# RWKV6 attention with an MLP on one core: round 0 turned by back-to-back transposes, and later rounds' w, k and r fetched in runs of steps and turned on VectorE

## The chip, the core and the metric

The kernel runs on one NeuronCore of a Trainium2 chip. A core has a matrix engine (TensorE, "PE" in the profile; its weight loads are "PEld"), a vector engine (VectorE, "DVE"), a scalar engine (ScalarE, "ACT"), a general engine (GpSimd, "POOL") and a queue engine (SyncE, "SP") that issues most transfers between HBM and the on-chip memory SBUF. 16 DMA engines carry the transfers. [...] Each engine runs its own instructions in order, and engines wait for one another by semaphores. The metric is device time in microseconds, the median of the runs of a kernel.

## The reference

The inputs r, k, v and w are float32 of [4 batches, 8 heads, 768 steps, 48 dimensions]. Attention is a recurrence over steps, followed by a layer norm and an MLP on 384 = 8 x 48 features:

```python
for t in range(S):
    kt, vt, rt, wt = (k[:, :, t], v[:, :, t], r[:, :, t], w[:, :, t])
    cur = np.einsum('bhd,bhe->bhde', u[None] * kt, vt)
    y[:, :, t] = np.einsum('bhd,bhde->bhe', rt, state + cur)
    state = wt[:, :, :, None] * state + np.einsum('bhd,bhe->bhde', kt, vt)
...
x = np.ascontiguousarray(attn_out.transpose(0, 2, 1, 3)).reshape(B, S, H * D)
xn = (x - mu) / np.sqrt(var + 1e-06) * g_ln
ch = np.maximum(xn @ w_ch1, 0.0) @ w_ch2
return (x + ch).astype(np.float32)
```

w_ch1 is [384, 1536] and w_ch2 is [1536, 384]. They arrive in float64, 8 bytes an element.

## The kernel before

The work is cut into 8 rounds, one for each batch and half of its 768 steps. A round has two units, one for each group of 4 heads, so a unit is 4 heads x 384 steps, and units 2n and 2n+1 belong to round n. Units 0 and 1 are round 0.

For the recurrence the kernel needs r, k and w with dimensions on the partitions and steps along the row: two heads share the 128 partitions, one from 0 and one from 64, so each tensor of a unit consists of two pairs of heads, each [128, 384]. In HBM the steps come first, so each pair has to be turned. `load` (L122) brings a tensor of a unit with steps on the partitions into a padded tile `nat` (three transfers of [128, 4, 48] each), and `turned` (L306) turns one pair: three PE transposes of 128x128 into PSUM and one copy to SBUF by ACT, into `wT` or `rkT`. For round 0 the rows are loaded by `load_rows` (L133) so that a partition holds three consecutive steps, and `turned` uses two 64-row products with the identity for each third of a pair. A product of float32 runs as two instructions on PE, a transpose as one.

A round then goes through six levels (0 to 5). In each, `quads` (L416) forms the products of k with r between neighbouring blocks of 1, 2, 4 ... 32 steps for both units (`a_ps`, 96 instructions), `grow` (L436) multiplies r and k by the decays that have come up to that block size (DVE, in place in `rkT`, so it waits for the level's products), and `keep` (L453) puts the wanted products into the matrix A by a mask. `totals` makes the decays by pairwise products of w. After level 5, `ends` turns k back (`kn`), `finish` copies the remainder, `states` (L509) makes the states at block ends (`kv` on PE, a chain on DVE), and `own_outputs` and `outputs` (L550, L565) give y. The term with u is r*k*u summed over dimensions: in rounds 0 and 1 by `products` (an elementwise product r*k, written `ruk`) and `product_sums` (PE, with u as the other side), later by `own_products` and `own_sums` from the untouched `nat` tiles; `own_term` multiplies it by v. DVE adds y and this term to x.

`moments` and `norm` (L602, L612) make xn, `turned_x` (L628) turns it (`xT`), and `mlp` (L640) is a generator of 24 steps of six PE instructions each: 12 for the hidden rows h (ACT applies the ReLU), and 12 for the output, whose sum with x DVE adds before SP stores it. The MLP of a round runs in the levels of the next two rounds.

The order on PE, ACT, DVE and POOL is the order in which the program states the calls. Transfers issued through `SP` are placed in the queue by a scheduler with its own estimate of the time; those through `SPO` keep the program's order. In the main loop, over `rnd` and `lev`, a level first does the states or outputs of the previous round, then `quads`, `grow` and `keep`; then `fill` (L697) deals the level's list of tasks out among MLP steps. `UNTIL` says how many MLP steps are done at the end of each level. Among the tasks are the turns of the next round: in round 2 at levels 3 to 5, in later rounds at levels 1 to 3, in the order w of both units, k and r of the first unit, k and r of the second. `norm` is a task of level 3, and `turned_x` of level 4.

The weights are converted while round 0 and 1 run: `fetch` brings a part in float64 words into one of four buffers with the tag "raw" ([128, 384, 2] words), `begin` (three ACT operations) takes it apart, and `join` (`shifted`, then `added`, on DVE) puts the float32 value together. The first MLP product needs three joined parts. `warm` issues idle products of zeros on PE between the steps of round 0.

Of the kernel before, what the change touches and what calls it, by code (L numbers as in the profile page):

```python
# [52 lines left out]
def kernel(  # L53
# [68 lines left out]
    def load(q, which="wkr", eng=SP):  # L122
        for nm in which:
            for c in range(TT):
                eng.dma_start(
                    out=nat[nm][q % 2][:, c, :, 0:D],
                    in_=steps({"w": w, "k": k, "r": r}[nm], q, c),
                )

    def flat(nm, q):  # L130
        return nat[nm][q % 2].rearrange("p c h d -> p (c h d)")

    def load_rows(nm, q, eng):  # L133

        b, f, g = units[q]
        src = {"w": w, "k": k, "r": r}[nm]
        eng.dma_start(
            out=flat(nm, q)[:, 0 : NH * TT * D].rearrange("p (h x) -> p h x", h=NH),
            in_=src[b, ts(g, NH), ds(f * RN, RN)].rearrange("h (p c) d -> p h (c d)", c=TT),
        )  # L140

    def load_v(q, eng=SP):
        vn[q] = p4.tile([P, TT, NH, D], F32, tag="v", name=f"v{q}")
# [148 lines left out]
    def warm(n, tag="m"):  # L292

        while n > 0:
            m = min(n, RN // P)
            ps = (ps_m if tag == "m" else ps_t).tile([P, RN], F32, tag=tag, name="idle")
            PE.matmul(
                ps[:, 0 : m * P], nought.broadcast_to([P, P]), nought.broadcast_to([P, m * P]),
                start=True, stop=True,
            )  # L300
            n -= m


    st, carry = {}, {}

    def turned(q, nm, pr):  # L306
        a = st.setdefault(q, {})
        if pr == 0:
            if nm == "w":
                if q % U == 0:  # L310
                    st["w"] = p1.tile([P, U, W], F32, tag="w", name=f"wT{q // U}")
                a["w"] = st["w"][:, q % U]
            elif "rk" not in a:

                rk = a["rk"] = p4.tile([P, 2, W], F32, tag="rkT", name=f"rkT{q}")
                a["r"], a["k"] = rk[:, 0], rk[:, 1]
        ps = ps_t.tile([P, RN], F32, tag="t", name=f"{nm}_ps{q}_{pr}")
        if q < U:

            for c in range(TT):  # L320
                for j in range(2):
                    at = ((2 * pr + j) * TT + c) * D
                    PE.matmul(
                        ps[ds(HP * j, HP), ts(c, P)], flat(nm, q)[:, ds(at, HP)], ident,
                        start=True, stop=True,
                    )
            ACT.copy(
                out=a[nm][:, ts(pr, RN)].rearrange("p (m c) -> p m c", c=TT),
                in_=ps.rearrange("p (c m) -> p m c", c=TT),
            )  # L330
            return
        for c in range(TT):
            PE.transpose(
                ps[:, ts(c, P)],
                nat[nm][q % 2][:, c, ts(pr, 2)].rearrange("p j d -> p (j d)"), ident,
            )
        ACT.copy(out=a[nm][:, ts(pr, RN)], in_=ps)
# [33 lines left out]

    def products(q, eng=DVE):
        a = st[q]
        if q < U:

            a["ruk"] = [
                p3.tile([P, RN], F32, tag="xn", name=f"ruk{q}_{pr}") for pr in pairs
            ]
            for pr in pairs:
                eng.tensor_tensor(  # L380
                    out=a["ruk"][pr], in0=a["r"][:, ts(pr, RN)], in1=a["k"][:, ts(pr, RN)],
                    op=ALU.mult,
                )
        else:
            ruk = p2.tile([P, NK, P], F32, tag="kn", name=f"ruk{q}")
            ruk = ruk.rearrange("p k t -> p (k t)")
            a["ruk"] = [ruk[:, ts(pr, RN)] for pr in pairs]
            eng.tensor_tensor(out=ruk, in0=a["r"], in1=a["k"], op=ALU.mult)

    def product_sums(q):  # L390
        b, f, g = units[q]
# [24 lines left out]
    def quads(q, lev):  # L416

        n = 1 << lev
        rnd, uu = divmod(q, U)
        if uu == 0:  # L420
            ps = ps_a.tile([P, 2, 512], F32, tag="a", name=f"a_ps{rnd}_{lev}")
            a_ps[rnd] = ps[:, :, 0 : W // 2].rearrange("s j (u k t) -> s j u k t", u=U, k=NK)
        K = st[q]["k"]
        R = st[q]["r"].rearrange("p (m q two n) -> p m q two n", m=NM, two=2, n=n)
        for c in range(NK):
            for i in range(2):
                for j in range(2):
                    m = 2 * c + i
                    rows = ds(HP * j, D)
                    PE.matmul(  # L430
                        a_ps[rnd][ds(C * (i ^ j), C), j, uu, c]
                        .rearrange("s (q n) -> s q n", n=n),
                        K[rows, ts(m, C)], R[rows, m, :, 1, :], start=True, stop=True,
                    )
# [301 lines left out]
    fetch(2)  # L736
    for nm in "wrk":
        run(each(turned, [u0], nm, pairs))
        warm(2)
    for nm in "wrk":  # L740
        POOL.memset(nat[nm][0][:, :, :, D:HP], 0.0)
    products(u0)
    quads(u0, 0)
    load(new[0], "wrk", SPO)
    grow(u0, 0)
    run(each(turned, [u1], "w", pairs))
    totals(0, DVE)
    warm(2)
    product_sums(u0)
    for nm in "rk":  # L750
        run(each(turned, [u1], nm, pairs))
        warm(2)
    for nm in "wrk":
        POOL.memset(nat[nm][1][:, :, :, D:HP], 0.0)
    products(u1)
# [3 lines left out]
    load_v(u0, SPO)  # L759
    load(new[1], "r", SPO)  # L760
    load_v(u1, SPO)
    load(new[1], "k", SPO)
    begin()
    begin()
    warm(3)
    grow(u1, 0)
    keep(0, 0)
    ahead = each(turned, new[:1], "wrk", pairs) + each(turned, new[1:], "wrk", pairs)
    for lev in range(1, NLEV):
        quads(u0, lev)  # L770
        quads(u1, lev)
        run(ahead[2 * lev - 2 : 2 * lev] if lev < NLEV - 1 else [])
        if lev in (2, 3):
            begin()
        warm(3 if lev < NLEV - 1 else 0)
        for which in ("rk",) if lev < NLEV - 1 else "kr":
            for q in (u0, u1):
                grow(q, lev, which)
        keep(0, lev)
# [11 lines left out]
    exchanged(u0)  # L791
    states(u1)
    product_sums(u1)
    join()
    own_term(u1, POOL)
    own_outputs(u0)
    warm(3, "t")
# [4 lines left out]
    own_outputs(u1, "m")  # L802
    outputs(u1)
    moments(0)
    begin()
    load(units_of(2)[0], "w", SPO)
    load(units_of(2)[1], "w", SPO)
    run(ahead[8:])
# [3 lines left out]
    warm(3)  # L812
    norm(0)
    begin()
    join()
    products(new[1])
    run(each(turned_x, [0], range(KC)))
# [11 lines left out]
    for rnd in range(1, NR + 1):  # L829
# [3 lines left out]
        for lev in range(NLEV):  # L833
# [37 lines left out]
                if lev in (4, 5):  # L871
                    own_term(now[lev - 4], POOL)
            if rnd == 2 and lev == 0:
                tasks += each(load_v, now) + each(load, new, "w")
            if rnd == 2 and lev == 2:
                for q in now:
                    take(DVE, q)
                    tasks += each(load, new[q % U :][:1], "kr")
            if rnd == 2 and lev in (3, 4):
                tasks += each(own_term, now[lev - 3 :][:1], [POOL])  # L880
            if rnd > 2 and lev < 2:
                tasks += each(load, new, ["w", "kr"][lev])
            first = 3 if rnd == 2 else 1
            if rnd > 1 and new and first <= lev < first + 3:
                m = lev - first
                tasks += each(turned, new[m - 1 : m], "kr", pairs) if m else each(
                    turned, new, "w", pairs
                )
            if rnd == 2:
                if lev == 0:  # L890
                    tasks += each(exchanged, old)
# [78 lines left out]
```

## Time and profile before

| | |
|---|---|
| median of 11 runs | 587.72 us (584.19 to 591.24) |
| the profiled execution, its own time | 589.4 us |
| its span | 587.4 us |
| PE products of the MLP (h_ps and o_ps), each | 576 instructions, 199.2 us busy |
| transposes of w, k, r with 128 columns (w_ps, k_ps, r_ps) | 84 each, mean 276 to 283 ns |
| copies of the turned pairs by ACT (wT, rkT) | 96, mean 477 to 478 ns |
| mask products kept by DVE (COPY_PREDICATED) | 32, mean 1198 ns |
| states by DVE (SCALAR_TENSOR_TENSOR) | 160, mean 258 ns |
| transfers, HBM read and written | 28.51 and 4.72 MB |
| mean granted PE clock | 0.991 of full |

The profile takes one execution. Busy time of PE counts from an instruction's start to its modelled end, and products overlap, so the mean of one is more than the distance from one start to the next; where the cost of a stretch matters, the distance between starts in the timeline is used. All instructions that go through the recording helper carry the line L49, so rows are told apart by the tiles they write and read. The page's second part cuts the span into 40 slices, each digit the busy share in tenths. A DMA share of 1 means that all 16 engines are moving packets.

### The profile page before, as it was taken

What the parts mean: (1) busy time and instruction counts of PE and PEld (TensorE: products, weight loads), DVE (VectorE), ACT (ScalarE), POOL (GpSimd) and SP (SyncE); (2) the same over time, 40 slices, a digit from 0 to 9 for tenths busy, and PEclk for the clock granted to TensorE, in tenths of its full rate; (3) what the DMA queues carried; (4) which work ended last, traced back from release to release, by engine and by line L of the source; (5) the groups of instructions that cost most, each with busy time, mean ns of one, the idle gap of its engine ahead of it and who ended that gap; (6) DMA issues with size and microseconds to landing.
All of it is one profiled execution on the core that took longest, in us unless ns stands there. A gap on an engine that the chain in (4) does not pass through costs nothing.

```text
span 587.4 us, 19224 instructions
## 1 busy us (share of the span) xinstructions
PE 575.0 (98%) x8644; PEld 385.6 (66%) x8644; DVE 273.9 (47%) x575; ACT 194.7 (33%) x426; POOL 90.9 (15%) x124
## 2 busy tenths in 40 slices
PE   9998989999999999999999999999999999999997
PEld 6776765666666666676666666666666665666554
DVE  3889779778265433444362443336244441130000
ACT  3568497402452225212423115412341015202200
POOL 6140020204250026000530008000320000000000
PEclk9998799999999999999999999999999999999999
DMA  9928697046213402340204302021000000000000
GB/s 230 192 85 170 138 262 161 2 90 133 53 36 81 91 15 42 57 93 25 55 3 93 66 29 41 2 54 38 15 3 2 15 29 2 1 15 28 0 15 27
DMA packets 114193, 36.53 MB, mean 62 GB/s; under 512 B 104768, under 2 KB 111040, under 8 KB 114112
## 3 DMA queue, kind: packets, MB, share of 16 engines
q1 hardware_dynamic: 112240, 34.72, 26.8%
q8 instruction: 68, 1.11, 0.8%
q10 hardware_dynamic: 1872, 0.59, 0.4%
q14 instruction: 13, 0.11, 0.1%
HBM read 28.51 MB, written 4.72 MB: 57 GB/s over the span
## 4 chain that ended last, share of the span: by engine, by line
PE 89%; ACT 5%; DVE 3%; DMA 1%; issue 1%; SPq 0%; ACTq 0%; DVEq 0%
PE o_ps L49 32%; PE h_ps L49 30%; PE a_ps L49 11%; PE y L49 4%; PE kv L49 2%; PE k_ps L49 2%; PE r_ps L49 2%; PE kn_ps L49 2%; PE w_ps L49 2%; PE xT_ps L49 1%; ACT rest L49 1%; PE idle L49 1%; PE own_ps L49 1%; ACT w_sb L49 1%; ACT rkT L49 1%
## 5 line engine op out<-in xcount | busy, mean ns | idle before, releaser
L49 PE MATMUL o_ps<-w_sb,h 128*128 128x384 f32 x576 | 199.2, 490 | 1.4 <-ACT h L49 0.9
L49 PE MATMUL h_ps<-xT,w_sb 128*128 128x384 f32 x576 | 199.2, 494 | 0.0
L49 PEld LDWEIGHTS h_ps<-xT,w_sb 128*128 128x128 f32 x576 | 105.8, 192 | 62.9 <-DVE w_sb L49 0.6
L49 PEld LDWEIGHTS o_ps<-w_sb,h 128*128 128x128 f32 x576 | 104.4, 190 | 62.6 <-ACT h L49 1.9
L49 DVE TENSOR_TENSOR rkT<-rkT,tot 128x768 f32<-128x768 f32 (+1 forms) x96 | 77.8, 853 | 38.9 <-issue 27.5
L49 ACT ACTIVATE h<-h_ps 128x384 f32<-128x384 f32 x96 | 46.8, 488 | 144.9 <-PE h_ps L49 144.7
L49 PEld LDWEIGHTS a_ps<-rkT 48*64 48x64 f32 x4608 | 72.3, 135 | 20.8 <-issue 15.3
L49 PE MATMUL a_ps<-rkT 48*64 48x32 f32 x4608 | 77.4, 220 | 0.3 <-issue 0.3
L49 DVE TENSOR_TENSOR o<-o_ps,x 128x384 f32<-128x384 f32 x24 | 13.4, 556 | 122.5 <-PE o_ps L49 122.4
L49 POOL TENSOR_TENSOR vo<-v,own 128x576 f32<-128x576 f32 x16 | 19.7, 1230 | 292.5 <-DVE own L49 252.5
L49 DVE SCALAR_TENSOR_TENSOR s<-s,decay,kv 128x48 f32<-128x48 f32 x160 | 29.3, 258 | 34.3 <-PE kv L49 34.3
L49 DVE COPY_PREDICATED A<-mask,a_ps 128x768 f32<-128x768 int8 x32 | 38.3, 1198 | 0.0
L49 DVE TENSOR_TENSOR x<-y,vo 128x288 f32<-128x288 f32 x32 | 13.1, 452 | 51.8 <-PE y L49 51.8
L49 ACT COPY rkT<-k_ps 128x384 f32<-128x384 f32 x32 | 14.3, 478 | 55.5 <-PE k_ps L49 55.5
L49 ACT ACTIVATE xT<-xT_ps,g_sb 128x384 f32<-128x384 f32 x24 | 13.7, 580 | 55.1 <-PE xT_ps L49 55.0
L49 ACT COPY rkT<-r_ps 128x384 f32<-128x384 f32 x32 | 14.6, 477 | 23.4 <-PE r_ps L49 23.4
L49 DVE TENSOR_SCALAR w_sb<-w_sb 128x384 f32<-128x384 f32 (+1 forms) x48 | 20.1, 419 | 0.8
L49 ACT COPY wT<-w_ps 128x384 f32<-128x384 f32 x32 | 14.3, 478 | 13.2 <-PE w_ps L49 8.8
L49 PE MATMUL r_ps<-ident,nat_r 128*128 128x128 f32 (+1 forms) x132 | 16.2, 277 | 2.6 <-ACT rkT L49 2.1
L49 DVE TENSOR_REDUCE own<-rk 128x12 f32<-128x576 f32 x12 | 9.0, 750 | 20.6 <-POOL rk L49 20.6
L49 ACT ACTIVATE rstd<-mv,eps 128x3 f32<-128x3 f32 x8 | 2.4, 296 | 48.7 <-DVE mv L49 48.6
L49 DVE TENSOR_TENSOR rkT<-rkT,wT 128x768 f32<-128x768 f32 x16 | 17.8, 1145 | 0.8 <-PE a_ps L49 0.8
(73 smaller groups left out, 521.6 us busy)
## 6 DMA issues: line engine op xcount, KB each, us to landing
raw<-in_moe_w_ch_dram SPq DMA_DIRECT2D x24, 384.0 KB, 4.1
v<-in_v_dram SPq DMA_DIRECT2D x48, 96.0 KB, 3.5
out_dram<-o SPq DMA_DIRECT2D x24, 192.0 KB, 2.4
nat_w<-in_w_dram SPq DMA_DIRECT2D x42, 96.0 KB, 3.0
nat_r<-in_r_dram SPq DMA_DIRECT2D x42, 96.0 KB, 2.9
nat_k<-in_k_dram SPq DMA_DIRECT2D x42, 96.0 KB, 2.8
vx<-v SPq DMA_DIRECT2D x28, 72.0 KB, 2.9
nat_r<-in_r_dram ACTq DMA_DIRECT2D x2, 288.0 KB, 5.1
```

The lines of the kernel that those rows point to most:

```text
L49: return lambda *args, **kw: self.tc.keep_in_program_order(f(*args, **kw))
```

## The change

In round 0, `turned` uses transposes: for each third of a pair first one over 128 columns, which puts the second head at partitions 64 to 127 and other data at 0 to 63, and then one over 64 columns that writes the first head over the latter. For unit 0 the second pair of each tensor is copied out by DVE and not by ACT. The idle products between these turns are gone; w of unit 1 is turned ahead of unit 0's level 0; the product r*k of a unit is one operation; unit 0's sums stand in level 1 in place of its idle products. One `join` moves from before unit 1's own term to behind the norm, with a second already there; a `begin` moves from behind the moments into level 4, and k of unit 3 is loaded behind two begins.

For rounds 3 to 7, `turned` and the loads of w are replaced by `stage` and `squares`. `stage` fetches a pair of heads into a buffer of the tag "raw": partition s of 32 holds the 12 consecutive steps 12s to 12s+11 of one head from its first dimension, 560 values in one run, and partition 32+s the same from dimension 32, so a head takes 64 partitions and one transfer. For the last head of the tensor, where the run would pass its end, two transfers are made and the missing corner cleared. `squares` turns a pair by one VectorE transpose of 32x32 squares, written with a stride of 12. A level's `stage` tasks come one level ahead of its `squares`. k and r are still loaded into `nat` too, for the own products; w is not.

```diff
@@ -139,6 +139,36 @@
             in_=src[b, ts(g, NH), ds(f * RN, RN)].rearrange("h (p c) d -> p h (c d)", c=TT),
         )
+    SQ = 32
+    NS = RN // SQ
+    ROW = (NS - 1) * D + SQ
+    staged = {}
+    def stage(q, nm, pr, eng=SP):
+        b, f, g = units[q]
+        src = {"w": w, "k": k, "r": r}[nm]
+        t = p4.tile([P, WC, 2], F32, tag="raw", name=f"{nm}_runs{q}_{pr}")
+        t = staged[q, nm, pr] = t.rearrange("p n two -> p (n two)")[:, 0 : NS * D]
+        for j in range(2):
+            first = src.offset + ((b * H + g * NH + 2 * pr + j) * S + f * RN) * D
+            if (q, pr, j) == (NU - 1, NP - 1, 1):
+                POOL.memset(t[P - SQ :, NS * D - SQ :], 0.0)
+                both = [(e, 1, ROW - e * (ROW - NS * D + SQ)) for e in range(2)]
+            else:
+                both = [(0, 2, ROW)]
+            for e, many, n in both:
+                eng.dma_start(
+                    out=t[ds(HP * j + SQ * e, SQ * many), 0:n],
+                    in_=bass.AP(
+                        tensor=src.tensor, offset=first + SQ * e,
+                        ap=[[SQ, many], [NS * D, SQ], [1, n]],
+                    ),
+                )
     def load_v(q, eng=SP):
         vn[q] = p4.tile([P, TT, NH, D], F32, tag="v", name=f"v{q}")
         for c in range(TT):
@@ -303,28 +333,39 @@
     st, carry = {}, {}
+    def turned_to(q, nm):
+        a = st.setdefault(q, {})
+        if nm == "w":
+            if q % U == 0:
+                st["w"] = p1.tile([P, U, W], F32, tag="w", name=f"wT{q // U}")
+            a["w"] = st["w"][:, q % U]
+        elif "rk" not in a:
+            rk = a["rk"] = p4.tile([P, 2, W], F32, tag="rkT", name=f"rkT{q}")
+            a["r"], a["k"] = rk[:, 0], rk[:, 1]
+        return a
+    def squares(q, nm, pr):
+        a = st[q] if pr else turned_to(q, nm)
+        DVE.transpose(
+            out=a[nm][:, ts(pr, RN)].rearrange("p (t s) -> p s t", s=NS),
+            in_=staged.pop((q, nm, pr)).rearrange("p (s d) -> p s d", s=NS)[..., 0:SQ],
+        )
     def turned(q, nm, pr):
-        a = st.setdefault(q, {})
-        if pr == 0:
-            if nm == "w":
-                if q % U == 0:
-                    st["w"] = p1.tile([P, U, W], F32, tag="w", name=f"wT{q // U}")
-                a["w"] = st["w"][:, q % U]
-            elif "rk" not in a:
-                rk = a["rk"] = p4.tile([P, 2, W], F32, tag="rkT", name=f"rkT{q}")
-                a["r"], a["k"] = rk[:, 0], rk[:, 1]
+        a = st[q] if pr else turned_to(q, nm)
         ps = ps_t.tile([P, RN], F32, tag="t", name=f"{nm}_ps{q}_{pr}")
         if q < U:
             for c in range(TT):
-                for j in range(2):
-                    at = ((2 * pr + j) * TT + c) * D
-                    PE.matmul(
-                        ps[ds(HP * j, HP), ts(c, P)], flat(nm, q)[:, ds(at, HP)], ident,
-                        start=True, stop=True,
+                for j in (1, 0):
+                    at = ((2 * pr + j) * TT + c) * D - HP * j
+                    PE.transpose(
+                        ps[0 : HP * (j + 1), ts(c, P)],
+                        flat(nm, q)[:, ds(at, HP * (j + 1))], ident,
                     )
-            ACT.copy(
+            (DVE.tensor_copy if q == 0 and pr else ACT.copy)(
                 out=a[nm][:, ts(pr, RN)].rearrange("p (m c) -> p m c", c=TT),
                 in_=ps.rearrange("p (c m) -> p m c", c=TT),
             )
@@ -371,21 +412,15 @@
     def products(q, eng=DVE):
         a = st[q]
         if q < U:
-            a["ruk"] = [
-                p3.tile([P, RN], F32, tag="xn", name=f"ruk{q}_{pr}") for pr in pairs
-            ]
-            for pr in pairs:
-                eng.tensor_tensor(
-                    out=a["ruk"][pr], in0=a["r"][:, ts(pr, RN)], in1=a["k"][:, ts(pr, RN)],
-                    op=ALU.mult,
-                )
+            ruk = p2.tile([P, TT, H, D], F32, tag="x", name=f"ruk{q}")
+            ruk = ruk.rearrange("p c h d -> p (c h d)")[:, 0:W]
         else:
             ruk = p2.tile([P, NK, P], F32, tag="kn", name=f"ruk{q}")
             ruk = ruk.rearrange("p k t -> p (k t)")
-            a["ruk"] = [ruk[:, ts(pr, RN)] for pr in pairs]
-            eng.tensor_tensor(out=ruk, in0=a["r"], in1=a["k"], op=ALU.mult)
+        a["ruk"] = [ruk[:, ts(pr, RN)] for pr in pairs]
+        eng.tensor_tensor(out=ruk, in0=a["r"], in1=a["k"], op=ALU.mult)
     def product_sums(q):
         b, f, g = units[q]
@@ -736,20 +771,15 @@
     fetch(2)
     for nm in "wrk":
         run(each(turned, [u0], nm, pairs))
-        warm(2)
     for nm in "wrk":
         POOL.memset(nat[nm][0][:, :, :, D:HP], 0.0)
     products(u0)
+    load(new[0], "wrk", SPO)
+    run(each(turned, [u1], "w", pairs))
     quads(u0, 0)
-    load(new[0], "wrk", SPO)
     grow(u0, 0)
-    run(each(turned, [u1], "w", pairs))
     totals(0, DVE)
-    warm(2)
-    product_sums(u0)
-    for nm in "rk":
-        run(each(turned, [u1], nm, pairs))
-        warm(2)
+    run(each(turned, [u1], "rk", pairs))
     for nm in "wrk":
         POOL.memset(nat[nm][1][:, :, :, D:HP], 0.0)
     products(u1)
@@ -759,9 +789,9 @@
     load_v(u0, SPO)
     load(new[1], "r", SPO)
     load_v(u1, SPO)
-    load(new[1], "k", SPO)
     begin()
     begin()
+    load(new[1], "k", SPO)
     warm(3)
     grow(u1, 0)
     keep(0, 0)
@@ -770,9 +800,12 @@
         quads(u0, lev)
         quads(u1, lev)
         run(ahead[2 * lev - 2 : 2 * lev] if lev < NLEV - 1 else [])
-        if lev in (2, 3):
+        if lev in (2, 3, 4):
             begin()
-        warm(3 if lev < NLEV - 1 else 0)
+        if lev == 1:
+            product_sums(u0)
+        elif lev < NLEV - 1:
+            warm(3)
         for which in ("rk",) if lev < NLEV - 1 else "kr":
             for q in (u0, u1):
                 grow(q, lev, which)
@@ -791,7 +824,6 @@
     exchanged(u0)
     states(u1)
     product_sums(u1)
-    join()
     own_term(u1, POOL)
     own_outputs(u0)
     warm(3, "t")
@@ -802,7 +834,6 @@
     own_outputs(u1, "m")
     outputs(u1)
     moments(0)
-    begin()
     load(units_of(2)[0], "w", SPO)
     load(units_of(2)[1], "w", SPO)
     run(ahead[8:])
@@ -812,6 +843,7 @@
     warm(3)
     norm(0)
     begin()
+    join()
     join()
     products(new[1])
     run(each(turned_x, [0], range(KC)))
@@ -871,21 +903,23 @@
                 if lev in (4, 5):
                     own_term(now[lev - 4], POOL)
             if rnd == 2 and lev == 0:
-                tasks += each(load_v, now) + each(load, new, "w")
+                tasks += each(load_v, now)
             if rnd == 2 and lev == 2:
                 for q in now:
                     take(DVE, q)
                     tasks += each(load, new[q % U :][:1], "kr")
             if rnd == 2 and lev in (3, 4):
                 tasks += each(own_term, now[lev - 3 :][:1], [POOL])
-            if rnd > 2 and lev < 2:
-                tasks += each(load, new, ["w", "kr"][lev])
+            if rnd > 2 and lev == 1:
+                tasks += each(load, new, ["kr"])
             first = 3 if rnd == 2 else 1
-            if rnd > 1 and new and first <= lev < first + 3:
+            if rnd > 1 and new and first - 1 <= lev < first + 3:
                 m = lev - first
-                tasks += each(turned, new[m - 1 : m], "kr", pairs) if m else each(
-                    turned, new, "w", pairs
-                )
+                turns = [(new, "w"), (new[:1], "kr"), (new[1:], "kr")]
+                if m >= 0:
+                    tasks += each(squares, *turns[m], pairs)
+                if m < 2:
+                    tasks += each(stage, *turns[m + 1], pairs)
             if rnd == 2:
                 if lev == 0:
                     tasks += each(exchanged, old)
```

## The prediction

> **What bounds the kernel now.** I read the page first: busy shares, slices, the chain that ended last.
>
> ```profile
> PE 575.0 (98%) x8644; PEld 385.6 (66%) x8644; DVE 273.9 (47%) x575; ACT 194.7 (33%) x426; POOL 90.9 (15%) x124
> PE   9998989999999999999999999999999999999997
> DMA  9928697046213402340204302021000000000000
> PE 89%; ACT 5%; DVE 3%; DMA 1%; issue 1%; SPq 0%; ACTq 0%; DVEq 0%
> ```
>
> PE is full and carries the chain; the transfers are nearly idle after the first quarter. So PE work taken out of a round shortens it, if nothing else takes PE's place. The timeline of PE shows how turns lie among the MLP's products, and where round 4 waits (a_ps at 224.3 starts its level 0, at 234.5 level 1, at 270.22 level 4):
>
> ```profile
> 238.37 2.10 PE L49 MATMUL h_ps<-xT,w_sb 128*128 128x384 f32 x6
> 240.31 0.82 PE L49 MATMUL w_ps<-ident,nat_w 128*128 128x128 f32 x6
> 240.96 2.10 PE L49 MATMUL h_ps<-xT,w_sb 128*128 128x384 f32 x6
> ...
> 270.22 1.60 PE L49 MATMUL a_ps<-rkT 48*64 48x32 f32 x96
> 271.75 0.55 PE L49 MATMUL xT_ps<-ident,xn 128*128 128x128 f32 x3
> ...
> 280.63 1.60 PE L49 MATMUL a_ps<-rkT 48*64 48x32 f32 x96
> ```
>
> From start to start six transposes take 0.65 us, so one turned pair 0.325. In level 4 the xT transposes stand directly behind the level's products, so PE goes no further until DVE has made xn. The DVE timeline puts xn in level 3:
>
> ```profile
> 265.05 1.47 DVE L49 BATCH_NORM_STATS2 stats<-x 128x6 f32<-128x384 f32 x3
> ...
> 267.55 1.26 DVE L49 TENSOR_SCALAR xn<-x,mv,rstd 128x384 f32<-128x384 f32 x3
> ```
>
> For transfers: the issues with their time to landing, and the fullest window (columns: PE, PEld, DVE, ACT, POOL busy, PE clock, mean share of 16 DMA engines, GB/s).
>
> ```profile
> raw<-in_moe_w_ch_dram SPq DMA_DIRECT2D x24, 384.0 KB, 4.1
> nat_w<-in_w_dram SPq DMA_DIRECT2D x42, 96.0 KB, 3.0
> ...
> 84.00:88.00 4.00, 4.00 (x95) 2.98 (x88) 3.86 (x5) 3.48 (x8) 1.76 (x1) 1.00 1.02 384
> ```
>
> 384 GB/s over 16 engines at a share of 1.02 is 23.5 GB/s for one busy engine, a third of the packets being small; single slices of that window show 430 to 461, or 27 to 29. I take 25.
>
> [...]
>
> **The change, part by part.**
> Round 0's turns: per tensor 12 products of two passes (24 instructions, 1.5 us) become 12 one-pass transposes at 0.108, 1.3 us: 0.2 saved, six times. Six pairs of idle products on zeros (0.63 us each) go. DVE takes three evictions; one product r*k of 128x768 (0.95) replaces two of 128x384 (1.21). Followed through: w is turned from 4.8, but ACT is held by its table load until 6.85, so r starts at 7.35; r and k are evicted by 10.85, w of unit 1 turned by 11.5, level-0 products until 12.4, grow 13.4, totals (2.6) 16.0, unit 1's product r*k 16.95, its grow and the mask product's start 17.9, which was 21.73. DVE, full from 20 to 60 us, keeps about 3.5 of these 3.8. The sums of unit 0 (1.2) replace a product r*k (0.65) in level 1. Three joins precede the first MLP product as before; the two behind the norm free 2 us ahead of the x sums. The begins are as many. k of unit 3 is issued behind two raws, some 1 us later, and first used near 45 us. Net: 3.5 gained; 5.5 if the joins' move counts in full; 5 lost if the transposes leave the clock halved from 8 to 20 us.
>
> Rounds 3 to 7: 60 turns leave PE, 60 x 0.325 = 19.5 us, with 60 ACT copies of 0.48 (off the path). DVE gets 60 transposes of 128x384. Its rows of that size take 0.40 to 0.56; I take 0.55, with 1.2 as the upper bound [...]. Ordinary rounds have DVE busy 5 to 10 of 20 us, so 12 more in 64 us are hidden when their data is there. In DVE's order they follow keep in levels 1, 2, 3; of level 3 they stand between the moments and the norm.
>
> SP loses 30 loads of w and issues 123 runs, some 0.5 us each: 24 for 6 in a round, 9 us more on a queue that mostly waits (its longest waits are those of the output stores for their sums on DVE). In SP's built order they stand between loads of v, k and r for later rounds and two copies vx; where a copy waits for its v to land ahead of the second group of k and r, up to 3 us a round are added, which I don't count. POOL clears three small corners for the last tiles, some 0.1 each, beside nothing that waits. What matters is what each run does. Its target has 64 rows, its source [2, 32, 560]; the built instruction carries outer sizes 64 and 2. [...] each with 32 rows of 2,240 B = 71.7 KB: 2.87 us at 25 GB/s, and all runs use the same two. On 16 engines it would be 0.36. A tile is two runs: 5.73; a level's four tiles 22.9. There are four raw buffers, so a tile is fetched only when a transpose has freed one. [...]
>
> **Where that goes.** Four tiles per level of 8 to 13 us can't keep up, and the transposes make DVE wait, with grow and the norm queued behind them. In an ordinary round, from its level-1 products: 6.15 until a transpose frees the first buffer (grow starts 2.0 later, takes 1.8, keep 1.9, one transpose), 3.05 from issue to landing beyond the own bytes (raw's 4.1 less 1.05), eight tiles of k and r 45.9, the v loads on the same engines 2.5, the last transpose and the norm 2.05: 59.7. Then PE does the rest of level 4 (8.9), level 5 (11.5) and level 0 (10.2, all from the starts of a_ps). Period 90.3, where now it is 67.8 (234.5 to 302.3): 22.5 more, for rounds 4, 5 and 6: 67. The next w is fetched within those 30 us.
> In rounds 2 and 3: w of round 3 lies early in SP's order and is there at 141.5, where the first transpose ends. Then five levels' tiles follow each other on the two engines: 141.5 - 3.5 + 3.05 + 114.5 + 2.5 + 2.05 = 260.1 at the norm of round 3, + 28.7 of PE = 288.8 at round 4's level 1, now 234.5: 54 more. Round 7 stages nothing and runs as now. About six long stalls cost PE a slow window each (3.4 us at half clock, 1.7): 10. Sum 67 + 54 + 10 = 131; the 19.5 saved is contained, since no turned level is in these PE pieces. Span 587.4 + 131 = 718; the profiled time lies 2.0 above its span, the median of the runs 1.7 below that time: 718 again.
>
> **Rivals.**
> A, on the other side: the runs spread over 16 engines [...]. Four tiles then take 2.9 us of transfer and are hidden: -19.5 - 3.5, so 565. For it: 64 target rows would spread, and the page's DMA row is nearly empty. It decides from where eight runs pass in the 11.2 us between two levels' transposes: under 1.4 us a run, that is about 4 engines.
> B: spread, and DVE is the bound. In level 3 grow starts 1.1 after the products and, with keep (2.8), moments (1.8), four transposes at 1.2 and the norm (1.5), ends at 12.0; PE, without its turns, comes to xT at 9.0. 3 us in each of five rounds: 580. Against it: at 0.55 the norm ends at 9.4, and DVE idles 4 to 7 us in most other levels.
> C: two engines, but each faster than 25 GB/s when alone: [...] at 23.5, 735.
> D: nothing moves (within 0.3%): would need a delay that just eats 23 us.
>
> **How the numbers follow.** Two engines: 0.84, of which C's spread of rates gives 690 to 735 and the errors of my chain 675 to 755 as its own range. A 0.12, B 0.03, D 0.01. The time is that of two engines, 718. To leave out no more than 2 in 10, with A and B outside, the range takes nearly all of the main case: 620 to 775. Faster by over 0.3% (about what a measurement of this kernel can tell from no change) 0.15, within 0.01, slower 0.84.
>
> **What will show it.** Right: runs landing a median of 10 us or more after issue; DVE's largest wait being on transfers of k and r runs; PE idle at xT behind DVE; PE share near 80%; windows of staged levels with the DMA share near 0.13 (2 of 16) and 50 GB/s; slow clock behind stalls; starts of level 1 some 90 us apart. Wrong: runs landing in 3 us and PE still full mean A. Transposes over 1 us with PE waiting for grow mean B. If DVE waits for runs but rounds stay under 80 us, the engines' rate or the serial order of levels is what I have wrong. A clock at half before 20 us would show in round 0, worth 5 us at most.

## The result: 743 us, and the profile after

The changed kernel takes 743.02 us (740.16 to 746.97, 12 runs), against 588.27 us for the kernel before (47 runs): a ratio of 1.263, with a 95% interval from 1.260 to 1.266. The profiled execution of the changed kernel has a span of 744.2 us, 156.8 more than before.

The page of the changed kernel: busy shares, PE's slices, its clock, the DMA engines' share, and the chain that ended last.

```profile
PE 578.2 (78%) x8378; PEld 381.3 (51%) x8378; DVE 320.3 (43%) x636; ACT 168.8 (23%) x363; POOL 94.4 (13%) x127
PE   8999999935497109995089970699717999999998
PEclk9898999986589558997579995799957999999999
DMA  9755834411133221412214122130221000000000
PE 48%; DMA 19%; issue 15%; SPq 7%; DVE 7%; ACT 2%; POOL 1%; DVEq 0%; ACTq 0%; POOLq 0%
```

PE was at 98%. It now has holes in every round that stages runs (2 to 6), with the clock down to half in them, and the chain runs through transfers for a fifth of the time. Yet the DMA row shows 1 to 2 tenths where PE stands still: the transfers that end the waits fill only a small part of the 16 engines.

The waits of PE and of DVE (total us, times, longest us):

```profile
PE xT_ps L49 <- DVE xn L49: 89.8, 4, 25.0
PE a_ps L49 <- DVE rkT L49: 44.4, 7, 18.5
PE kn_ps L49 <- DVE rkT L49: 17.5, 1, 17.5
...
DVE rkT L49 <- DMA r_runs<-in_r_dram: 99.0, 20, 5.3
DVE rkT L49 <- DMA k_runs<-in_k_dram: 73.0, 16, 9.3
```

PE waits 151.7 us for DVE, about as much as the kernel lost, and DVE waits 172 us for runs of k and r. For runs of w it waits 4.3 us once. PE's idle time as a whole went from 12.4 us (587.4 less 575.0) to 166.0 (744.2 less 578.2). Its busy time rose by 3.2 us although the turns are gone: the products behind a stall run in part at half clock (mean clock 0.79 from 375.16 to 386.06, for one). One ordinary round, round 4, on DVE's timeline (start, duration, then idle time before the row and what ended it):

```profile
331.93 0.87 DVE L49 STREAM_TRANSPOSE rkT<-k_runs 128x384 f32<-128x384 f32 x1 [3.12 <-DMA k_runs<-in_k_dram]
337.94 0.86 DVE L49 STREAM_TRANSPOSE rkT<-r_runs 128x384 f32<-128x384 f32 x1 [5.15 <-DMA r_runs<-in_r_dram]
343.83 0.85 DVE L49 STREAM_TRANSPOSE rkT<-r_runs 128x384 f32<-128x384 f32 x1 [5.03 <-DMA r_runs<-in_r_dram]
...
355.35 0.84 DVE L49 STREAM_TRANSPOSE rkT<-k_runs 128x384 f32<-128x384 f32 x1 [5.37 <-DMA k_runs<-in_k_dram]
361.12 0.85 DVE L49 STREAM_TRANSPOSE rkT<-k_runs 128x384 f32<-128x384 f32 x1 [4.93 <-DMA k_runs<-in_k_dram]
...
373.00 0.85 DVE L49 STREAM_TRANSPOSE rkT<-r_runs 128x384 f32<-128x384 f32 x1 [5.04 <-DMA r_runs<-in_r_dram]
...
373.90 1.26 DVE L49 TENSOR_SCALAR xn<-x,mv,rstd 128x384 f32<-128x384 f32 x3
```

From one tile of two runs to the next it is 5.8 to 6.0 us (the 11.5 us from 343.83 to 355.35 are taken up below). 143.4 KB for each of two engines in 5.95 us is 24.1 GB/s an engine. The norm stands behind the last transpose, and PE behind the norm. On PE's timeline of the same round:

```profile
346.70 2.78 PE L49 MATMUL a_ps<-rkT 48*64 48x32 f32 x96 [3.58 <-DVE rkT L49]
374.44 1.25 PE L49 MATMUL xT_ps<-ident,xn 128*128 128x128 f32 x3 [24.95 <-DVE xn L49]
...
386.06 1.60 PE L49 MATMUL a_ps<-rkT 48*64 48x32 f32 x96
```

A window in which nearly nothing but these runs is under way (columns as before: PE, PEld, DVE, ACT and POOL busy, PE clock, DMA share, GB/s):

```profile
164.00:171.00 7.00, 0.00 (x0) 0.00 (x0) 0.85 (x1) 0.00 (x0) 0.00 (x0) 0.50 0.13 49
```

A share of 0.13 is 2 of 16 engines, and 49 GB/s is twice the 24.1 above.

### The profile page after: what moved, and what is told of

It is laid out like the page before. It is cut to its first block, busy times and chain, and to the rows that moved or that the text cites. A ratio compares the mean times of both kernels' runs of the same rounds, so it can differ in the third digit from the quotient of the medians.

```text
span 744.2 us, 18836 instructions
## 1 busy us (share of the span) xinstructions
PE 578.2 (78%) x8378; PEld 381.3 (51%) x8378; DVE 320.3 (43%) x636; ACT 168.8 (23%) x363; POOL 94.4 (13%) x127
## 4 chain that ended last, share of the span: by engine, by line
PE 48%; DMA 19%; issue 15%; SPq 7%; DVE 7%; ACT 2%; POOL 1%; DVEq 0%; ACTq 0%; POOLq 0%
PE h_ps L49 18%; PE o_ps L49 16%; DMA r_runs<-in_r_dram 12%; PE a_ps L49 5%; DMA k_runs<-in_k_dram 5%; SPq L125 4%; DVE rkT L49 3%; SPq L164 2%; PE y L49 2%; DVE A L49 1%; DMA v<-in_v_dram 1%; PE kv L49 1%; POOL rk L49 1%; PE xT_ps L49 1%; DVE w_sb L49 1%
## 5 line engine op out<-in xcount | busy, mean ns | idle before, releaser
L49 PE MATMUL o_ps<-w_sb,h 128*128 128x384 f32 x576 | 208.0, 512 | 1.0 <-ACT h L49 1.0
L49 PEld LDWEIGHTS o_ps<-w_sb,h 128*128 128x128 f32 x576 | 110.6, 199 | 70.8 <-issue 7.7
L49 PE MATMUL a_ps<-rkT 48*64 48x32 f32 x4608 | 85.0, 229 | 46.8 <-DVE rkT L49 44.4
L49 PEld LDWEIGHTS a_ps<-rkT 48*64 48x64 f32 x4608 | 79.2, 145 | 68.2 <-DVE rkT L49 49.6
L49 PE MATMUL xT_ps<-ident,xn 128*128 128x128 f32 x72 | 15.5, 323 | 90.3 <-DVE xn L49 89.8
L49 PEld LDWEIGHTS xT_ps<-ident,xn 128*128 128x128 f32 x72 | 10.4, 159 | 99.0 <-DVE xn L49 92.4
L49 DVE STREAM_TRANSPOSE rkT<-r_runs 128x384 f32<-128x384 f32 x20 | 17.0, 848 | 99.0 <-DMA r_runs<-in_r_dram 99.0
L49 DVE STREAM_TRANSPOSE rkT<-k_runs 128x384 f32<-128x384 f32 x20 | 17.1, 853 | 74.8 <-DMA k_runs<-in_k_dram 73.0
L49 PE MATMUL kn_ps<-ident,rkT 128*128 128x128 f32 x96 | 14.8, 291 | 18.4 <-DVE rkT L49 17.5
L49 PEld LDWEIGHTS kn_ps<-ident,rkT 128*128 128x128 f32 x96 | 11.8, 148 | 24.1 <-DVE rkT L49 18.1
```

The costliest lines, as they stand in the source:

```text
L49: return lambda *args, **kw: self.tc.keep_in_program_order(f(*args, **kw))
```

## The experiments

Ratios are those of the medians to the kernel before, measured beside each; intervals are 95%.

### One number: how many engines a run gets

Four kernels change only how a run's 64 rows are described. `order16` and the two with groups keep the 123 transfers, their bytes and their 2,240-byte rows, but put rows where they don't belong; `rows32` puts every row in its place.

```diff
 # order16
-                        ap=[[SQ, many], [NS * D, SQ], [1, n]],
+                        ap=[[NS * D, 32], [SQ, many], [1, n]],
 # groups4 (groups8: 8 * NS * D - SQ, 8 and 8)
-                        ap=[[SQ, many], [NS * D, SQ], [1, n]],
+                        ap=([[16 * NS * D - SQ, 4], [NS * D, 16], [1, n]] if many == 2
+                            else [[NS * D, SQ], [1, n]]),
 # rows32: two transfers of 32 rows for each run
-                both = [(0, 2, ROW)]
+                both = [(e, 1, ROW) for e in range(2)]
```

> The change with the source's two outer sizes in the other order, [32, 2, 560] for [2, 32, 560]: the same 123 transfers, bytes and packets, but rows of the two halves land interleaved, so values stand in wrong places of w, k and r. Two-engine theory: 32 is now the outer size of the source, 64 of the target, so 16 engines: 565 (562 to 571), runs landing in about 3 us. Rivals: a transfer's size, its row length or the number of descriptors sets its rate, not its outer sizes: 743 as before; SP's issues matter: 3 us or more below the version with 32 rows.

> The change with the source as [8, 8, 560] (eight groups of eight rows, each 128 bytes short of the next row's place, so the values are not the right ones), the same 123 transfers and packets. Two-engine theory, read as a rule of the outer sizes: 8 engines, a run 0.74 us where it was 2.97, four tiles 5.9 us in a level of 8 to 13: hidden, 567 (563 to 573). Rival, an outer size that isn't a multiple of 16 confines to two engines or one: 743 or more.

> The change with the source as [4, 16, 560] in the same manner, values not the right ones, the same 123 transfers and packets. Two-engine theory: 4 engines, a tile 2.97 us, four tiles 11.9 us against levels of 10.6 in the mean: nearly at the edge that the prediction put at about four engines. Round period 96.5 - 8 x 2.97 - 2.8 (half of the wait for the copy vx) - 2.7 (half clock behind stalls) = 67, so 585 (572 to 605). Rival, as for 8: 743.

> The change, with each run of 64 rows issued as two transfers of 32 rows, so that 32 stands as outer size on both sides. Two-engine theory: each transfer spreads over 16 engines, a tile passes in about 0.75 us where it took 5.9, DVE no longer waits for runs, and the time is 588.3 - 19.5 (turns off PE) - 1.8 (earlier start of round 2) = 567 (563 to 575; the upper part if SP's doubled issues, 240 by about 0.5 us, delay stores or loads). Rival, DVE's transposes (0.85 us) or the order of the work hold PE up, not the engines: 580 or more, with PE waiting on DVE. Rival, short scattered rows are slow whatever the engines: still near 743.

| kernel | outer size of the source | us | ratio |
|---|---|---|---|
| the change | 2 | 743.02 | 1.263 (1.260 to 1.266) |
| groups4 | 4 | 620.50 | 1.052 (1.046 to 1.058) |
| groups8 | 8 | 575.71 | 0.975 (0.970 to 0.980) |
| order16 | 32 | 575.12 | 0.974 (0.968 to 0.979) |
| rows32 | 32, twice the transfers | 580.59 | 0.984 (0.979 to 0.990) |

The loss follows the outer size; number, bytes and row length of the transfers are the same in the first four. Two dimensions of an access pattern in the other order are worth 168 us. In `order16` DVE's waits for r fall from 99.0 to 2.4 us, and those for k are gone from the list. PE's busy share and the time of the r runs from issue to landing (least, median, most):

```profile
PE 556.5 (97%) x8378; PEld 368.4 (64%) x8378; DVE 315.8 (55%) x636; ACT 168.6 (29%) x363; POOL 92.6 (16%) x127
...
DMA to landing us min/median/max: 2.3/2.9/4.6
```

In `groups4` DVE's timeline shows tiles 2.9 to 3.2 us apart, half of the 5.95 of the change, as four engines should give:

```profile
290.15 0.84 DVE L49 STREAM_TRANSPOSE rkT<-r_runs 128x384 f32<-128x384 f32 x1 [2.38 <-DMA r_runs<-in_r_dram]
293.09 0.85 DVE L49 STREAM_TRANSPOSE rkT<-r_runs 128x384 f32<-128x384 f32 x1 [2.10 <-DMA r_runs<-in_r_dram]
```

The share of the DMA engines rises with the outer size. A window of `groups4` while runs pass:

```profile
226.00:232.00 6.00, 6.00 (x49) 3.42 (x48) 0.35 (x1) 0.58 (x1) 0.00 (x0) 0.87 0.26 96
```

One of `groups8`, and the same window of `order16`:

```profile
250.50:253.50 3.00, 3.00 (x102) 2.21 (x101) 1.38 (x3) 0.00 (x0) 0.00 (x0) 1.00 0.44 123
```

```profile
250.50:253.50 3.00, 3.00 (x102) 2.22 (x101) 1.38 (x3) 0.00 (x0) 0.00 (x0) 1.00 0.75 221
```

0.26 is four of 16 engines, and 96 GB/s is four times 24. 0.44 stays under the half that eight engines can fill (where loads of v pass too, it rises to 0.62), and 0.75 lies above it. In these two, SP issues a run every 0.6 to 0.8 us and the engines are not full, so the number of engines is bounded by the share and not read from it.

The changed kernel holds a comparison of its own. In round 6 the last head of the tensor is fetched by two transfers of 32 rows, because its run would pass the end. DVE's timeline of the change there, for k:

```profile
547.87 0.85 DVE L49 STREAM_TRANSPOSE rkT<-k_runs 128x384 f32<-128x384 f32 x1 [3.36 <-DMA k_runs<-in_k_dram]
551.16 0.84 DVE L49 STREAM_TRANSPOSE rkT<-k_runs 128x384 f32<-128x384 f32 x1 [2.44 <-DMA k_runs<-in_k_dram]
```

The second pair of k, with one such head, comes 3.3 us behind the first instead of 5.9, that of r 3.2 us, and this round is 5 us shorter than the two before it (91.6 against 96.5 and 96.1 between starts of level 1).

All four came slower than I expected, and outside the ranges: `order16` 575 for 565 (562 to 571), `groups8` 576 for 567 (563 to 573), `rows32` 581 for 567 (563 to 575), and `groups4` 620 for 585 (572 to 605). For the first three, most of it is missing early: from round 2's level 0 to round 4's level 1 their traces take 122.4, 121.3 and 127.2 us, against 122.8 before, where I had taken 7.8 us less. `rows32` also came to the 580 of its rival, in which PE waits for DVE (2.1 us for the norm, 3.0 for the states). `groups4` missed by 35. Its rounds are 74.3 and 74.2 us apart, not 67: PE still waits for the norm in four rounds (26.7 us in all, 7.8 at most), and its mean clock is 0.945 where `order16` has 0.985. I had set both waits and clock to nothing there. What separates `rows32` from `order16` is not settled: the intervals only just part, the two traces differ by 1.8 us, and in that of `rows32` PE waits 3.0 us for the states of round 3 instead of 1.5. The kept trace of `rows32` is also the fastest of its five executions (575.99 us at a mean clock of 0.994); the other four take 580 to 583 us at 0.976 to 0.982, where `order16` has 0.982 to 0.985, so part of the difference is clock.

### What the serial order cost: the copies vx, and w

```diff
 # vx_by_pool
                 for q in now:
-                    load_vx(q)
+                    load_vx(q, POOL)
 # w_spread
-                both = [(0, 2, ROW)]
+                both = [(e, 1, ROW) for e in range(2)] if nm == "w" else [(0, 2, ROW)]
```

> The change with two engines left as they are, and the copies vx of rounds 2 to 7 made by POOL instead of SP transfers. Theory: in each round SP stood on a copy vx until v had landed, with the second group of runs behind it (11.5 us between two tiles where 5.9 is the rule); without it 5.6 us a round go for rounds 4 to 6, and 0 to 2 for round 3: 743 - 17 to 19 = 725 (720 to 732). Rival, the two engines are the only limit and the wait is hidden in their backlog: 743 within 4.

> The change, with only the runs of w issued as two transfers of 32 rows each (16 engines); k and r stay on two. Theory: in rounds 4 to 6 w passes behind the last k and r while PE does levels 4, 5 and 0, so it costs nothing there and the periods stay at 91 to 97; between rounds 2 and 4 w of round 4 stands in one queue between two sets of k and r, 8 runs x 2.97 = 23.8 us, which go, and the loads behind it come earlier by up to 9: 743 - 24 to 33 = 715 (708 to 722). Rival, the loss goes by the bytes on the two engines, of which w is a third: 743 - 52 = 691. Rival, only k and r matter: 743 within 4.

`vx_by_pool` takes 728.27 us, ratio 1.234 (1.226 to 1.242), 14.8 us less than the change. In the change, SP's timeline shows why: the copy vx waits for v, and the next runs of k stand behind it.

```profile
331.05 9.26 SPq L175 DMA_DIRECT2D v<-in_v_dram  x3
344.83 1.35 SPq L181 DMA_DIRECT2D vx<-v  x2
346.29 2.75 SPq L164 DMA_DIRECT2D k_runs<-in_k_dram  x4
```

So 11.5 us lie between the tiles at 343.83 and 355.35. With POOL's copies the same two tiles on DVE's timeline are 7.0 us apart:

```profile
340.92 0.84 DVE L49 STREAM_TRANSPOSE rkT<-r_runs 128x384 f32<-128x384 f32 x1 [5.07 <-DMA r_runs<-in_r_dram]
...
347.95 0.84 DVE L49 STREAM_TRANSPOSE rkT<-k_runs 128x384 f32<-128x384 f32 x1 [0.88 <-DMA k_runs<-in_k_dram]
```

Its level-1 starts lie 91.0, 91.8 and 86.0 us apart, 5.5, 4.3 and 5.6 less than in the change. The expectation held (720 to 732), at its weak end: 17 to 19 us were forecast.

`w_spread` takes 734.47 us, ratio 1.246 (1.243 to 1.250): 8.5 us less, where I expected 24 to 33. The half on ordinary rounds held: 96.5, 96.2 and 91.9 us apart, so w is hidden there. The other half fell. The norm of round 3 comes at 268.20 instead of 280.25, 12 us earlier, not 24 to 33: with w early, the next runs of k are still issued at 213.43 only (227.75 in the change), since the buffers are freed by the transposes of w, and these stand behind level 1's mask product on DVE until 212.52. So about half of the 23.8 us that w's transfers take had been hidden: in the change DVE finds three of the four tiles there at 213.72, and waits 4.3 us for the fourth. Neither rival fits (691, or 743 within 4).

### Round 0 alone

`round0_only` has the change's round 0 and its moved joins, begins and sums, and the loads and turns of before in rounds 3 to 7:

```diff
-                turns = [(new, "w"), (new[:1], "kr"), (new[1:], "kr")]
-                if m >= 0:
-                    tasks += each(squares, *turns[m], pairs)
-                if m < 2:
-                    tasks += each(stage, *turns[m + 1], pairs)
+                tasks += each(turned, new[m - 1 : m], "kr", pairs) if m else each(
+                    turned, new, "w", pairs
+                )
```

> Only the change's first part (round 0, joins, begins, product r*k, sums moved); rounds 3 to 7 load and turn w, k and r as before. Prediction: 3.5 us faster than before, its bounds 5.5 faster to 5 slower. The traces of the change and of its first variants put the start of round 2's level 0 at 104.5 to 110.0 where it was 111.7, so 1.7 to 7 us, depending on how long PE's clock stays at half; so 584.5 (581 to 587) against 588.3, ratio 0.988 to 0.997. Rival, the stretch at half clock near 21 to 26 us, [...] eats all of it: ratio 0.998 to 1.003.

586.38 us beside 590.09, ratio 0.994 (0.991 to 0.997): 3.5 us gained, with an interval of 1.7 to 5.4. In this part the clock is what varies. The window of 20 to 28 us in the kernel before (the third number from the end is PE's clock):

```profile
20.00:28.00 8.00, 7.91 (x266) 6.02 (x270) 7.61 (x8) 4.80 (x11) 1.71 (x2) 1.00 0.88 144
```

The same window in the change:

```profile
20.00:28.00 8.00, 7.83 (x143) 6.67 (x144) 5.33 (x5) 2.97 (x8) 1.51 (x2) 0.58 0.70 142
```

Unit 0's mask product starts at 18.08 in the change, 3.65 earlier than before. But PE then runs at half clock from about 21.3 to 28, and level 5 starts at 34.33, where it started at 34.40. `round0_only` shows half clock for some 3.4 us there, and its level 5 starts at 32.06. Its program is that of the change up to there. So is that of nine other runs of this document, `idle_back` apart. In these eleven traces the half clock between 20 and 34 us lasts some 3.4 us in eight, 6.7 in the change and 10.2 in `groups8`, and is absent in `rows32`. Level 5 starts between 31.58 (`rows32`) and 35.28 (`groups8`). So the stretch varies from execution to execution, and no single trace gives the worth of this part; the medians do.

### What is left in round 3, and a version faster than both

In `order16` a round from 4 on is 64.2 us, 3.6 less than the 67.8 of before: 12 pairs at 0.30. Round 3 gave nothing back: 61.9 us from level 1 to level 1, against 60.6. From round 2's level 0 to round 3's level 1 it is 60.5 against 62.2, so 1.8 us and not 3.6. PE's timeline of `order16` there:

```profile
195.94 1.60 PE L49 MATMUL a_ps<-rkT 48*64 48x32 f32 x96
199.54 1.89 PE L49 MATMUL xT_ps<-ident,xn 128*128 128x128 f32 x6 [2.00 <-DVE xn L49]
...
208.49 1.60 PE L49 MATMUL a_ps<-rkT 48*64 48x32 f32 x96
```

PE's level 3 is only 5.6 us long here, four transposes stand ahead of the norm, and PE waits 2.0 us. From 195.94 to 208.49 the clock is 0.86, and the level takes 12.55 us, where it took 8.48. `norm_first` is `rows32` with the norm ahead of them:

```diff
-                    tasks += each(norm, [rnd - 1])
+                    tasks = each(norm, [rnd - 1]) + tasks
```

> The version with two transfers of 32 rows, and in level 3 the norm ahead of the DVE transposes. Theory: what was left of the loss in round 3 was the norm behind four transposes of 0.74 to 0.85 (xT came 2.0 us late, and a window at half clock followed, 4 us in all); with the norm first that wait is gone and the ratio falls from 0.984 to about 0.975 (0.968 to 0.982). Rival, SP's doubled issues hold rows back in round 3: stays at 0.984.

573.76 us beside 590.09, ratio 0.973 (0.968 to 0.977): faster than the kernel before and than `rows32` (0.984). PE's timeline has no wait in that place, and the level takes 8.47 us at full clock:

```profile
200.52 1.60 PE L49 MATMUL a_ps<-rkT 48*64 48x32 f32 x96
202.05 0.87 PE L49 MATMUL xT_ps<-ident,xn 128*128 128x128 f32 x6
...
208.99 1.60 PE L49 MATMUL a_ps<-rkT 48*64 48x32 f32 x96
```

In the traces round 3 is 59.1 us long, where `rows32` has 62.1: 2.9 of the 6.8 us between the medians. The rest is not explained.

Two further edits, each on top of it, brought no gain that can be measured.

```diff
 # round2_earlier: runs and transposes of round 2 a level earlier
-            first = 3 if rnd == 2 else 1
+            first = 2 if rnd == 2 else 1
 # idle_back: the idle products on zeros again
         run(each(turned, [u0], nm, pairs))
+        warm(2)
...
             product_sums(u0)
-        elif lev < NLEV - 1:
+        if lev < NLEV - 1:
             warm(3)
```

> Two transfers of 32 rows, norm first, and round 2's runs and DVE transposes in levels 2 to 4 instead of 3 to 5. Theory: with the transposes in level 5 DVE is full from the end of round 2 on, the states wait and PE waits 3.0 us for them in round 3, with a window at half clock behind it (some 1.7); a level earlier DVE has room: 573.8 - 3 to 5, ratio 0.9726 - 0.005 to 0.008 = 0.966 (0.961 to 0.972). Rival, the transposes then crowd the own products in level 2 and 3 of round 2 and only move the wait: 0.971 to 0.976.

> Norm first, and the idle products on zeros put back: a pair behind each of unit 0's three turns and three calls' worth (0.8 us) in level 1. Theory: the stretch at half clock between 20 and 31 us, which the change has and the kernel before has not (6.8 us long in the trace of the change, about 3.4 in that of norm first), [...] with the idle products back the clock stays at full there, worth half of 3.4 to 6.8, less about 0.8 of PE time: 573.8 - 1 to 2.5, ratio 0.969 to 0.971. Rival, the half clock [...] only moves: 0.972 to 0.976 and a stretch at half clock elsewhere.

`round2_earlier`: 574.50 us, ratio 0.976 (0.973 to 0.978). The 3.0 us wait for the states is gone, and PE waits 3.8 us for DVE at the turns of k (1.0 in `norm_first`) and 2.5 us for an output sum instead. So the wait moved, as the rival said; that the own products are what it was moved by is not shown. `idle_back`: 573.43 us, ratio 0.975 (0.971 to 0.979). In its trace the clock is full from 16 to 40 us, and 0.72 from 40 to 46, some 3.4 us at half clock. That fits the rival by which it only moves, but one trace doesn't show it: `rows32` has no half clock before 40 us without the idle products either. What brings the stretch about is not shown.

### The transpose by itself

```diff
-            out=a[nm][:, ts(pr, RN)].rearrange("p (t s) -> p s t", s=NS),
+            out=a[nm][:, ts(pr, RN)].rearrange("p (s t) -> p s t", s=NS),
```

> As the version with [32, 2, 560], but the DVE transpose writes its squares side by side and not with a stride of 12 (values in wrong places). It measures the transpose alone: 0.85 us with the stride; if the stride is what costs, 0.4 to 0.5 us; if the 32x32 squares themselves are slow, still 0.85. Time as the strided version's, 571 to 577, or up to 4 less if round 3's late norm goes with it.

DVE's group for the transposes of k in `order16` (busy us, mean ns):

```profile
L49 DVE STREAM_TRANSPOSE rkT<-k_runs 128x384 f32<-128x384 f32 x20 | 15.4, 845 | 0.0
```

The same group in `flat_squares`:

```profile
L49 DVE STREAM_TRANSPOSE rkT<-k_runs 128x384 f32<-128x384 f32 x20 | 10.6, 558 | 0.9 <-DMA k_runs<-in_k_dram 0.9
```

The square transpose itself takes 0.56 us, a little more than the 0.4 to 0.5 that I expected; writing with a stride of 12 adds 0.29. The one execution took 569.1 us (order16: 573.1 to 576.9), and in it PE waits 1.1 us for the norm instead of 2.0.

## Why the prediction was right, step by step

**The mechanism.** Two engines for each run, the transposes waiting for them, the norm behind the transposes and PE behind the norm: each link is in the profile of the change, and the four outer sizes show that the first is the cause of the loss. That a source beginning with a 2 puts a run on two engines was my estimate: no trace of the kernel before showed it. The runs bear it out: for outer sizes of 2 and 4 the rate of tiles and the share (0.13 and 0.26) give 2 and 4 engines. For 8 and 32 the shares of 0.44 and 0.75 fit 8 and 16 without giving the number, so the 8 and the 16 of the expectations remain estimates. The target had 64 rows in each of these kernels; what its outer size does was not shown.

**A run's price.** Taken 2.87 us at 25 GB/s, measured 2.97 at 24.1; at the window's mean of 23.5 it would have been 3.05. The single slices of 27 to 29 GB/s an engine that led me to 25 were a poor guide: they are 0.1 us long and scatter from 163 to 492 GB/s for all engines, while pieces of 0.5 us of the same window move 288 to 424, which is 26.5 an engine at most.

**Ordinary rounds.** My sum gave 90.3 us; measured 96.5, 96.1 and 91.6, together 80.7 us more than before against my 67. The term that failed is the one I named and did not count: the wait of the copies vx for v, which I put at up to 3 us. It cost 4.3 to 5.6 a round (`vx_by_pool`); with it gone the first two periods are 91.0 and 91.8. The part from the norm to level 5 took 10.9 us, not 8.9, because PE runs at half clock behind the stall (0.79 in the mean); my lump of 10 us for six stalls was meant for this. It took 3.4 us at half clock for each; the trace of before has one stretch of that length (49.25 to 52.66) and one twice as long (62.90 to 69.73). Behind the stall of round 4 PE has some 5.2 us of work at half clock: its clock is at half from 345.5 to 379.7, and it starts again at 374.44.

**Rounds 2 to 4.** I had level 1 of round 4 at 288.8; it started at 311.20, so 76.7 us late and not 54. This is the largest error. The first run of k was issued at 145.88, where my sum has 138.0, so I took too early a start by 8 us. 20 tiles at 0.2 more make 4. And between the last w (220.19) and the first k (236.43) lie 16.2 us instead of 5.9, another 10: 16 loads of `nat_k` and `nat_r` passed on SP between 207.59 and 227.75, slowly, behind the runs of w; with these spread (`w_spread`) 14 such loads take 10.5 us. I had counted the loads of v there, not those of k and r. That five levels' tiles follow each other on the two engines held in the trace; but `w_spread` shows that it isn't all that sets this stretch, since without w's share only half of its time comes back.

**The sum.** 76.7 + 80.7 - 0.6 behind round 7 is 156.8, where I had 54 + 67 + 10 = 131. The 25 us missing are mostly sizes of waits, in the places that I had named; the loads of k and r are the one that I hadn't.

**Signs foretold.** PE share near 80%: 78%. DMA share 0.13 and 50 GB/s in staged windows: 0.13 and 49. Starts of level 1 some 90 us apart: 91.6 to 96.5. DVE's largest waits on runs of k and r: 172 us. Landing over 10 us: the page gives no landing time for these runs in the change. In round 4 SP issued the second runs of the two k tiles at 346.89 and 348.43, and the transposes that waited for them start at 355.35 and 361.12, 8.5 and 12.7 us later; for the r tiles behind them it is 17.4 and 15.4. A median over all runs stays unread.

**Rival A**, the runs on more engines, became true when they were spread: I gave it 565, and `order16` lies 15.7 us under the kernel beside it, not 23. Two terms were too large: a pair's turn gives 0.30 us back, not 0.325, and rounds 2 and 3 gave 1.8 and nothing. Its edge, under 1.4 us a run, was well placed: with four engines (1.5 us a run, from tiles 3 us apart) the kernel still loses 5%, with an outer size of 8 (0.74 by the same division, if that is eight engines) nothing. **Rival B** is the reason for round 3, but in one round and not five: the transpose takes 0.85 us, between my 0.55 and 1.2, and decides only where PE's level 3 is short. 0.55 is about what it takes without the stride. **Rival C**, two engines at another rate, is the main case with a different price: at 24.1 GB/s my sums give some 9 us more, 727, so the rate explains a third of the miss and the waits above the rest.

**Round 0.** Predicted 3.5 us gained, measured 3.5 (1.7 to 5.4). The half clock that I feared from 8 to 20 us came from 21 to 28, and in the profiled execution of the change it took the gain of round 0 nearly whole by level 5. In `rows32` there is none before 110 us. That the forecast was met to a tenth is luck, since the interval is 3.7 us wide, and the start of level 5 differs by as much between executions.

## What to carry to other kernels

Look at the outer dimension of a transfer's source before its bytes: here runs with a target of 64 rows passed at a DMA share of 0.13 and 49 GB/s where the source's pattern begins with a 2, and at 0.75 and 221 GB/s in a window of `order16`, where it begins with 32. When engines look idle and a consumer still waits on transfers, divide the GB/s by what one engine moves in a full window: here 49 by 23.5, which is two. And look for a copy in the queue that waits for a landing: here the loads behind vx were held up with it, which cost 4.3 to 5.6 us a round, since they were the bottleneck.

## What was not expected of the hardware

The transpose of a 128x384 float32 tile in squares on DVE took 0.56 us in `flat_squares`, and 0.85 in `order16`, which writes its output with a stride of 12 elements (48 bytes). In `order16`, a wait of PE by 2.0 us went with a level 4.1 us longer (12.55 for 8.48) and a stretch at half clock (0.86 in the mean over that level); with the norm first both are gone (8.47). And the stretch at half clock in round 0 was no fixed cost of the program: in eleven traces with the same round 0 it was absent, or some 3.4, 6.7 or 10.2 us long, each time close to a multiple of 3.4.
